# First batch's keys and values in six sets of 96 positions, q products in quarter tiles, idle products half as many, and a new set of ordering draws

## The chip, the core and the metric

The kernel runs on one core of a Trainium2 chip. Five engines work side by side, each through its own list of instructions in order, and meet at semaphores: TensorE (PE, matrix products into PSUM), VectorE (DVE), ScalarE (ACT), GpSimd (POOL) and SyncE (SP, which here only starts transfers). Sixteen DMA engines move data between HBM and SBUF. The metric is the device time of one execution in microseconds (us). Times named "us into the span" count from the first instruction of the profiled execution.

## The reference

Eight batches of eight heads, 576 positions, head dimension 64, all in float32. Attention without a softmax, an RMS norm per head, then four experts of two layers whose outputs are weighted by normalised probabilities and added up:

```python
def _attn_ref(q, k, v, g_norm) -> np.ndarray:
    kv = np.einsum('bhsd,bhse->bhde', k, v)
    out = np.einsum('bhsd,bhde->bhse', q, kv)
    rms = np.sqrt(np.mean(out * out, axis=-1, keepdims=True) + 1e-06)
    return (out / rms * g_norm).astype(np.float32)
...
    p = domain_probs / (domain_probs.sum(-1, keepdims=True) + 1e-09)
    out = np.zeros((N, D), dtype=np.float32)
    for e in range(E):
        h = np.maximum(x @ w1[e], 0.0)
        out += p[:, e:e + 1] * (h @ w2[e])
```

Here x has N = 4608 rows (8 x 576) of D = 512, w1 is 4 x 512 x 1024 and w2 is 4 x 1024 x 512. The sum over positions in `kv` has no order, so the 576 positions of a head may be cut into sets in any way, as long as k and v are cut alike.

## The kernel before

**Stages.** The rows are worked on in nine chunks of 512: the first 512 positions of each batch, and one chunk made of the 64 left over from each. Four experts times nine chunks make 36 steps s. Step s holds the first layer of one chunk (`up`, for s = 0 `up_plain`) and, beside it, the second layer (`down`, `down_deep`) of the chunk before. Most of these products are built with Strassen-like sums of blocks, which DVE and POOL form (line 563) and which ACT and DVE gather (lines 1432, 1440, 1760, 1768). All layer products are issued by one helper, `halves_of` (line 540): one product is split into two of 64 columns of weights each.

**How instructions show.** A float32 product stands in the trace as two weight loads (PEld) and two MATMUL records (PE), so 18 products of a source line are 36 records of each kind. A transpose through PE is one record of each kind.

**The opening (`opening`, line 860 on).** The first batch has a path of its own, since nothing else can run yet. It goes through four pairs of heads, hp = 0 to 3. For each:

- q, k and v of the pair are loaded by three transfers of 288 KB on SP's queue. All have the two heads one above the other on the 128 partitions: partition 64 h + p holds the nine positions 9 p to 9 p + 8 of head h, 9 x 64 numbers.
- `turns` (line 890): four transposes of q into an `ab` bank, which ACT copies out (line 895).
- `key_values` (line 905): nine sets of 64 positions; for each set one product per head, 64 rows by 64 columns, so 18 products, head 0 in the upper left quarter of the array and head 1 in the lower right. They gather in two banks, one `u2` and one `u1`. A last transpose (line 909) turns the ninth set of q. ACT and DVE copy the result out (lines 924, 921).
- `attend` (line 944), called twice: q times kv. For pairs 0 and 1 a call is eight products with 64 columns of weights (quarter tiles); for pairs 2 and 3 it is four products with 128 columns (`wide`). The result lies in halves of the two `db` banks (kind `raw`).
- `scaled`: squares on ACT (line 819), their sum on DVE (826), root and inverse (786 to 798), scaling on DVE (838); then four transposes back (`turn_x`, line 964), and ACT copies them out as a quarter of chunk 0 (line 970).

`up_plain` is the first layer of chunk 0 for expert 0, in the plain way: eight results i = 0 to 7, each gathering four pairs hp in one of the `u1` and `u2` banks, with 512 moving columns (the records "128x512"). Results 0 to 3 may begin as soon as pair 0 is there. The attention of the later batches (`attention`) loads k and v as 120 and 96 positions per set (`rows_of`); its products stand in line 1092, those with q in line 1117, the sums of squares in 1159 and 1165.

**Idle products.** Before the first data lands and in gaps of the opening up to key -1.99, PE runs `idle` (line 1921) on the identity matrix: four products of 64 x 64 x 64 into a free `ab` bank.

**Order.** The order of all instructions on all engines is worked out before the program is emitted, by a planner (`Plan`) in Python. Each operation has a key (its place in the steps), a cost per engine in us, and a due time. The planner runs a model of the engines, the transfers and the buffers, and at each moment an engine takes the operation that is due first among those that are ready. Due times are shifted by pseudo-random draws; `DEALS` names, for each step, the numbers of the draws that apply. An operation on a `raw` half waits in the model for others on these halves (`op.halves`, `seen`, `filled`). None of these numbers is read by the chip: they only set the order in which each engine's list is written.

**Weights.** Each expert's w1 and w2 are loaded while the expert before still runs. From expert 1 on some sums of weights are formed by ACT negating a block (line 636) and a transfer that adds HBM data on top.

Of the kernel before, what the change touches and what calls it, by code (L numbers as in the profile page):

```python
# [26 lines left out]
class Op:  # L27
    def __init__(self, key, cost, fn, reads, writes, kb, port):
        self.key, self.cost, self.fn, self.kb, self.port = key, cost, fn, kb, port
        self.outs = list(writes)  # L30
        self.bufs = list(dict.fromkeys(list(reads) + self.outs))
        self.deps = {}
        self.start = self.end = self.eng = None
        self.marks = self.seed = None
        self.wide, self.wants = {}, 0
        self.early = self.gang = self.opens = False
        self.halves = any(b.kind == "raw" for b in self.bufs)
# [5 lines left out]
class Plan:  # L43
# [20 lines left out]
    SLOW = 6.5  # L64
    SPREADS, SPREADS_PE, SHARES = (1.0, 2.0, 4.0), (0.0, 0.5, 1.5), (1.0, 0.2, 0.05)
# [42 lines left out]
    def prepare(self, slots, later, idle, idle_banks, idle_until):  # L108
# [50 lines left out]
        self.seen = self.filled = 0.0  # L159
# [74 lines left out]
    def ready(self, op, eng, front):  # L234
# [37 lines left out]
    def run(self, until):  # L272
# [3 lines left out]
        while self.left:  # L276
# [6 lines left out]
            for eng in todo:  # L283
# [35 lines left out]
                if eng == "PE" and busy[eng] <= t and 1.6 <= t and front < idle_until:  # L319
# [3 lines left out]
                    if spare is not None:  # L323
# [4 lines left out]
                        busy[eng] = op.end  # L328
# [14 lines left out]
    def begin(self, op, eng):  # L343
# [19 lines left out]
        if op.halves and eng == "PE":  # L363
            self.filled = max(self.filled, op.end)
        elif op.halves:
            self.seen = max(self.seen, op.end)
# [49 lines left out]
def kernel(  # L416
# [387 lines left out]
    def scaled(key, name, raw, n, x, blocks, by_half=False):  # L804
# [11 lines left out]
        for r in range(2):  # L816
# [6 lines left out]
            )  # L823
# [9 lines left out]
        for r in range(2):  # L833
# [19 lines left out]
            )  # L853
        return done

    x_part = [Buf(None, f"x0_{hp}") for hp in range(NPAIR)]
    opened = []

    def opening(key, span, rem):
# [9 lines left out]
        J = S // D  # L869
        qTs, kvs, lefts = {}, {}, []  # L870
        for hp in range(NPAIR):
            n = f"{b}_{hp}"
            loaded = {}
            for t, src, kb in zip("qkv", (q, k, v), (
                    (172, 194, 290), (183, 150, 150), (237, 400, 150), (172, 150, 172))[hp]):
                loaded[t] = Buf("big", f"{t}{n}")
                load(
                    key - 1 + 0.1 * hp, loaded[t], lambda t=loaded[t]: t.ap[:, 0:J * D],
                    src[b, 2 * hp:2 * hp + 2].rearrange("h (p j) d -> (h p) (j d)", j=J), kb,
                )  # L880
# [11 lines left out]
            plan.add(at(hp), {"PE": 0.54}, turns, reads=[qt], writes=[bank])  # L892
# [8 lines left out]
            def key_values(eng, bank=kbank, kt=kt, vt=vt, qt=qt):  # L901
                for j in range(J):
                    for r in range(2):
                        half, cols = slice(r * D, (r + 1) * D), slice(j * D, (j + 1) * D)
                        nc.tensor.matmul(  # L905
                            bank[r].ap[half, 0:D], lhsT=kt.ap[half, cols], rhs=vt.ap[half, cols],
                            start=(j == 0), stop=(j == J - 1), skip_group_check=True,
# [3 lines left out]
            plan.add(at(hp), {"PE": 1.3}, key_values, reads=[qt, kt, vt], writes=kbank)  # L911
# [38 lines left out]
            plan.add(  # L950
                at(hp + 0.4), {"PE": 0.26 if wide == D else 0.52}, attend, reads=[qT, kv_own], holds=[kv], writes=[raw])
            plan.add(
                at(hp + 0.4), {"PE": 0.26 if wide == D else 0.52}, lambda eng, attend=attend: attend(eng, other=1),
                reads=[qT, kv_other], holds=[kv], parts=[raw])
# [11 lines left out]
            plan.add(at(hp + 1), {"PE": 0.64}, turn_x, reads=[x], writes=[bank])  # L966
# [8 lines left out]

        n = f"{b}_r"
# [3 lines left out]
        def attend_rem(eng):  # L980
# [9 lines left out]
            at(NPAIR), {"PE": 1.07}, attend_rem,  # L990
            reads=list(kvs.values()) + list(qTs.values()) + lefts, writes=rawr)
# [11 lines left out]
        plan.add(at(NPAIR + 1), pe(4, P, 1), turn_xrem, reads=[xr], writes=[xb])  # L1003
# [16 lines left out]
    def attention(b, key, span, rem):  # L1020
# [26 lines left out]
        for s in range(2):  # L1047
# [64 lines left out]
            def attend(eng, raw=raw, rest=rest, kv=kv, qt=qt):  # L1112
# [9 lines left out]
            plan.add(  # L1122
                at(2 * s + 1.0), {"PE": 1.23}, attend, reads=[qt, kv], writes=raw + rest,
                early=True, gang=True,
            ).wide = {**{b: FIRST for b in raw}, **{b: S - FIRST for b in rest}}
# [29 lines left out]
        def total(eng):  # L1155
# [15 lines left out]
        plan.add(  # L1171
            when, {"PE": 1.23}, total, reads=both + [xs], writes=[ss]).wide = {ss: wide}
# [315 lines left out]
    def up_plain(s, e, c, key, span):  # L1488
# [4 lines left out]
        for i in range(8):  # L1493
            uh, a, u = i // 4, i // 2 % 2, i % 2
            bank = Buf("u1" if a == 0 else "u2", f"up{s}_{i}")
            for hp in range(NPAIR):
# [3 lines left out]
                def product(eng, w=w, bank=bank, dh=dh, kt=kt, ut=2 * a + u):  # L1500
# [9 lines left out]
                    **({"parts": [bank], "after": begun} if hp else {"writes": [bank]}),  # L1510
# [407 lines left out]
    def idle(bank):  # L1918
        for r in range(4):
            half = slice(r % 2 * D, (r % 2 + 1) * D)  # L1920
            nc.tensor.matmul(bank[half, 0:D], lhsT=ident[half, half], rhs=ident[half, half])  # L1921
# [54 lines left out]
```

## Time and profile before

| | |
|---|---|
| median of 3 runs | 1638.32 us (1638.09 to 1638.54) |
| the profiled execution, device time | 1638.29 us |
| its span, first to last instruction | 1636.5 us |
| PE busy | 1627.3 us, 99% of the span |
| DVE busy | 1317.3 us, 80% |
| ACT busy | 971.9 us, 59% |
| POOL busy | 625.7 us, 38% |
| mean granted TensorE clock | 0.999 |

A group in the profile gives line, engine, operation, what is written and read, shapes, count, and the busy time; in brackets stands the idle time before it and what ended it. The chain of waits follows the work that ended last back to the start: its rows give start, length in us, and the engine, tile and line. In a table by stages a row is the stretch, its length, the busy time, the count, the granted clock, the busy share of the DMA engines and GB/s. MATMUL records are pipelined, and each one's length holds some 0.2 us of its way through the array, so the pace is read from start to start (as in the chain), not from the mean of one.

### The profile page before, as it was taken

How to read it: one execution, taken by the hardware profiler on the slowest of the kernel's cores; microseconds unless marked ns; L12 is line 12 of the kernel's file. 1: busy time of each engine (PE TensorE's matmuls, PEld its weight loads, DVE VectorE, ACT ScalarE, POOL GpSimd, SP SyncE). 2: the span in 40 equal slices, each digit the busy share in tenths (PEclk: the TensorE clock that was granted, in tenths of full speed). 3: DMA queues.
4: the chain of work that ended last, by engine and by line, in shares of the span. 5: the costliest groups of instructions: out<-in, count | busy, mean ns of one | idle time of the engine just before them, and what ended most of it. 6: DMA issues, size and time to landing. Idle time of an engine off the chain costs nothing.

```text
span 1636.5 us, 66139 instructions
## 1 busy us (share of the span) xinstructions
PE 1627.3 (99%) x28692; PEld 1555.0 (95%) x28692; DVE 1317.3 (80%) x2211; ACT 971.9 (59%) x2462; POOL 625.7 (38%) x618
## 2 busy tenths in 40 slices
PE   9999999999999999999999999999999999999999
PEld 5698889888999999999999999999999999999997
DVE  6877777788889878977988887778889877787776
ACT  4465555565566666656666665665666666566653
POOL 4122424333343454433354533344254443333332
PEclk9999999999999999999999999999999999999999
DMA  9888777744764435444675543334577544444442
GB/s 234 225 186 248 183 215 209 173 147 173 236 166 131 118 95 154 118 108 116 181 178 136 130 111 102 116 104 118 144 186 181 120 113 118 118 115 108 118 105 53
DMA packets 225596, 240.96 MB, mean 147 GB/s; under 512 B 100890, under 2 KB 165274, under 8 KB 225306
## 3 DMA queue, kind: packets, MB, share of 16 engines
q1 hardware_dynamic: 201690, 199.96, 40.4%
q0 software_dynamic: 23616, 36.78, 15.0%
q8 instruction: 225, 3.69, 0.9%
q14 instruction: 65, 0.53, 0.1%
HBM read 162.21 MB, written 74.47 MB: 145 GB/s over the span
## 4 chain that ended last, share of the span: by engine, by line
PE 97%; DMA 1%; DVE 1%; SPq 0%; issue 0%; ACT 0%; POOL 0%; DVEq 0%; POOLq 0%; ACTq 0%
PE u L540 47%; PE db L540 31%; PE ab L540 15%; PE ab L1092 1%; DMA big<-in_moe_w_dram 1%; PE ab L1117 1%; PE ab L1159 0%; PE db L1117 0%; DMA big<-roots 0%; SPq L569 0%; PE u L905 0%; PE ab L1921 0%; PE db L944 0%; DVE xf L563 0%; DMA small<-in_q_dram 0%
## 5 line engine op out<-in xcount | busy, mean ns | idle before, releaser
L563 DVE TENSOR_TENSOR big<-big,big 128x256 f32<-128x256 f32 (+1 forms) x522 | 478.2, 932 | 28.1 <-ACT big L1396 13.6
L540 PE MATMUL u<-xf,big 128*64 128x128 f32 x6784 | 493.8, 273 | 0.0
L540 PE MATMUL db<-big,big 128*64 128x128 f32 (+1 forms) x5648 | 434.0, 290 | 0.4 <-DVE big L563 0.4
L540 PEld LDWEIGHTS u<-xf,big 128*64 128x64 f32 x6784 | 398.7, 137 | 2.9 <-issue 0.8
L540 PE MATMUL u<-xf,w1y 128*64 128x128 f32 x5304 | 395.4, 273 | 0.1
L540 PEld LDWEIGHTS db<-big,big 128*64 128x64 f32 x5648 | 339.8, 137 | 25.3 <-DVE big L563 0.9
L540 PEld LDWEIGHTS u<-xf,w1y 128*64 128x64 f32 x5304 | 313.5, 137 | 5.1 <-issue 1.0
L563 POOL TENSOR_TENSOR big<-big,big 128x256 f32<-128x256 f32 (+1 forms) x162 | 187.4, 1158 | 255.6 <-DVE big L563 110.6
L1440 DVE TENSOR_TENSOR big<-u,snap 128x256 f32<-128x256 f32 x440 | 185.2, 421 | 122.9 <-PE u L540 81.1
L1432 ACT ACTIVATE snap<-u 128x256 f32<-128x256 f32 x490 | 187.1, 382 | 161.9 <-PE u L540 142.1
L1432 ACT ACTIVATE big<-u 128x256 f32<-128x256 f32 x440 | 167.4, 382 | 71.8 <-PE u L540 54.0
L563 POOL TENSOR_TENSOR big<-big 128x512 f32<-128x512 f32 (+1 forms) x82 | 100.8, 1230 | 193.8 <-DVE big L563 99.2
L1760 ACT ACTIVATE snap<-db 128x256 f32<-128x256 f32 (+1 forms) x256 | 90.0, 352 | 106.1 <-PE db L540 88.2
L1396 ACT ACTIVATE big<-big 128x1024 f32<-128x1024 f32 x125 | 131.7, 1054 | 13.1 <-DVE big L563 7.6
L563 DVE TENSOR_TENSOR big<-big 128x512 f32<-128x512 f32 (+1 forms) x160 | 122.3, 772 | 2.4 <-PE db L540 1.2
L1768 DVE TENSOR_TENSOR big<-ab,snap 128x256 f32<-128x256 f32 x168 | 70.9, 422 | 63.9 <-ACT snap L1760 43.9
L1432 ACT ACTIVATE u<-u 128x256 f32<-128x256 f32 x245 | 90.7, 370 | 52.7 <-PE u L540 39.3
L1605 POOL DMA_DIRECT2D out_dram<-big x104 | 93.8, 1229 | 36.5 <-ACT big L1581 23.1
L540 PE MATMUL ab<-kv,big 128*64 128x128 f32 x1504 | 104.6, 273 | 0.0
L540 PE MATMUL ab<-big,big 128*64 128x128 f32 (+1 forms) x1384 | 96.9, 275 | 0.0
L540 PEld LDWEIGHTS ab<-kv,big 128*64 128x64 f32 x1504 | 87.2, 137 | 0.0
L540 PEld LDWEIGHTS ab<-big,big 128*64 128x64 f32 x1384 | 80.5, 137 | 1.2
(213 smaller groups left out, 2231.1 us busy)
## 6 DMA issues: line engine op xcount, KB each, us to landing
xf<-x SPq DMA_DIRECT2D x104, 512.0 KB, 3.6
xf<-x_h SPq DMA_DIRECT2D x85, 256.0 KB, 3.3
xf<-x SPq DMA_DIRECT2D x78, 256.0 KB, 3.8
x<-xf SPq DMA_DIRECT2D x36, 512.0 KB, 4.4
out_dram<-big POOLq DMA_DIRECT2D x68, 256.0 KB, 6.1
big<-in_moe_w_dram SPq DMA_DIRECT2D x30, 512.0 KB, 5.8
big<-in_moe_w_dram POOLq DMA_DIRECT2D x18, 512.0 KB, 7.6
x_h<-big SPq DMA_DIRECT2D x17, 512.0 KB, 4.1
```

The lines of the kernel that those rows point to most:

```text
L540: nc.tensor.matmul(out_[cols], lhsT=lhsT[:, cols], rhs=rhs, **kw)
L563: lambda eng: adder(eng).tensor_tensor(out=out_(), in0=a(), in1=b(), op=op),
L1092: nc.tensor.matmul(bank.ap[o * D:(o + 1) * D, r * D:(r + 1) * D], lhsT=ks[r], rhs=vs[r], start=(j == r == 0), stop=(j == len(sets[0]) - 1) ...
L1117: nc.tensor.matmul(to[o].ap[cols, 0:width], lhsT=kv.ap[half, cols], rhs=qt.ap[half, r * S + at_:r * S + at_ + width],)
L1396: lambda eng: nc.scalar.activation(out=b.ap[:], in_=b.ap[:], func=ACT.Relu),
L1432: lambda eng: nc.scalar.activation(out=where(), in_=ps.ap[:, 0:HN], func=ACT.Copy),
L1440: lambda eng: nc.vector.tensor_tensor(out=block(whole, a, t), in0=src.ap[:, 0:HN], in1=add_.ap[:], op=ALU.add),
L1605: nc.gpsimd.dma_start(out=dst, in_=cell(i)[parts, :], accum_op=ALU.add)
L1760: lambda eng: nc.scalar.activation(out=where(), in_=group_of(ps.ap), func=ACT.Copy),
L1768: lambda eng: nc.vector.tensor_tensor(out=cell(tq, dq), in0=group_of(src.ap), in1=group_of(add_.ap), op=ALU.add,),
```

## The change

Five things change.

- k and v of the first batch are loaded as six sets of 96 positions: partition p of 96 holds positions 6 p to 6 p + 5 of both heads, side by side. q is loaded as before.
- `key_values` follows: six sets, two heads, 12 products of 96 rows by 64 columns instead of 18 of 64 by 64.
- `attend` uses products with 64 columns of weights for all four pairs.
- `idle` is one call of `halves_of`: two products of 128 rows, 64 columns of weights and 128 moving columns, instead of four of 64 x 64 x 64.
- The planner: costs of the opening's products are set anew; an operation on `raw` halves now waits for other engines' work on the same bank; going between the opening's kinds of products and the others costs 0.11 us in the model (`SWITCH`, `turns`); results 1 and 3 of `up_plain` begin after the last pair's `key_values` (`first_kv`); and `DEALS` holds other draws for steps -3 to 15 and for 22, 23, 29 and 32.

```diff
-        -3: (61,), -2: (96, 339), -1: (17, 340), 0: (41, 337, 607, 846, 1010), 1: (145, 260, 617, 782,
...
+        -2: (178,), -1: (141,), 0: (175, 256, 724, 986, 1100), 1: (79, 362, 728, 792, 1183), 2: (54, 360,
...
-        if op.halves:
-            when = max(
-                when, self.seen + self.TO_PE if eng == "PE" else self.filled + self.AFTER_PE)
+        for bank in op.halves:
+            for e, end in self.halved[bank].items():
+                if e != eng:
+                    when = max(when, end + (
+                        self.AFTER_PE if e == "PE" else self.TO_PE if eng == "PE" else self.OTHER))
...
+            if eng == "PE":
+                op.end += self.SWITCH[op.turns] if op.turns != self.turned else 0.0
+                self.turned = op.turns
...
-        J = S // D
+        J, SETS = S // D, 6
+        ROWS = S // SETS
...
+                else:
+                    load(
+                        key - 1 + 0.1 * hp, loaded[t],
+                        lambda t=loaded[t]: t.ap[0:ROWS, 0:2 * SETS * D].rearrange(
+                            "p (h x) -> p h x", h=2),
+                        heads.rearrange("h (p j) d -> p h (j d)", j=SETS), kb,
+                    )
...
-                for j in range(J):
+                for j in range(SETS):
                     for r in range(2):
-                        half, cols = slice(r * D, (r + 1) * D), slice(j * D, (j + 1) * D)
+                        half, at = slice(r * D, (r + 1) * D), (r * SETS + j) * D
                         nc.tensor.matmul(
-                            bank[r].ap[half, 0:D], lhsT=kt.ap[half, cols], rhs=vt.ap[half, cols],
-                            start=(j == 0), stop=(j == J - 1), skip_group_check=True,
+                            bank[r].ap[half, 0:D], lhsT=kt.ap[0:ROWS, at:at + D],
+                            rhs=vt.ap[0:ROWS, at:at + D],
+                            start=(j == 0), stop=(j == SETS - 1), skip_group_check=True,
                         )
...
-            raw, wide = Buf("raw", f"raw{n}"), D if hp < 2 else P
+            raw, wide = Buf("raw", f"raw{n}"), D
...
-                    **({"parts": [bank], "after": begun} if hp else {"writes": [bank]}),
+                    **({"parts": [bank], "after": begun} if hp else {
+                        "writes": [bank], "after": first_kv if i in (1, 3) else ()}),
...
     def idle(bank):
-        for r in range(4):
-            half = slice(r % 2 * D, (r % 2 + 1) * D)
-            nc.tensor.matmul(bank[half, 0:D], lhsT=ident[half, half], rhs=ident[half, half])
+        halves_of(bank[:, 0:P], ident[:], rhs=ident[:])
```

More of the change, by code (lines that the diff above doesn't have):

```diff
@@ L36, in __init__ @@
         self.early = self.gang = self.opens = False
-        self.halves = any(b.kind == "raw" for b in self.bufs)
+        self.halves, self.turns = (), False
 BANKED = ("u1", "u2", "db", "ab")
@@ L327, in run @@
                         op.fn = lambda eng, bank=self.slots[kind][spare[1]]: idle(bank)
-                        busy[eng] = op.end
+                        busy[eng], self.turned = op.end, False
                         self.free[kind].remove(spare)
@@ L362, in begin @@
             self.worked += op.cost[eng]
[L363 to L366, printed above, removed]
+        for bank in op.halves:
+            self.halved[bank][eng] = max(self.halved[bank].get(eng, 0.0), op.end)
         if op.port:
@@ L822, in scaled @@
                 reads=[raw[r][0]], parts=[x],
-            )
+            ).halves = (r,) if by_half else ()
         plan.add(
@@ L948, in attend @@
                             )
[L950 to L954, printed above, removed]
+            for other, own in enumerate((kv_own, kv_other)):
+                op = plan.add(
+                    at(hp + 0.4), {"PE": 0.27},
+                    lambda eng, attend=attend, other=other: attend(eng, other=other),
+                    reads=[qT, own], holds=[kv], **{"parts" if other else "writes": [raw]})
+                op.halves, op.turns = (0, 1), True
             x = Buf("big", f"xg{n}")
@@ L1169, in total @@
                     )
-        plan.add(
-            when, {"PE": 1.23}, total, reads=both + [xs], writes=[ss]).wide = {ss: wide}
+        op = plan.add(when, {"PE": 1.13}, total, reads=both + [xs], writes=[ss])
+        op.turns, op.wide = True, {ss: wide}
         def root(eng):
```

37 lines of the change are left out of this document (22 added, 15 removed), and 10 rows, old and new, of the table DEALS.

## The prediction

> **What bounds the kernel now.** I read the page first: its busy times, then the chain of waits by engine.
>
> ```profile
> PE 1627.3 (99%) x28692; PEld 1555.0 (95%) x28692; DVE 1317.3 (80%) x2211; ACT 971.9 (59%) x2462; POOL 625.7 (38%) x618
> ...
> PE 97%; DMA 1%; DVE 1%; SPq 0%; issue 0%; ACT 0%; POOL 0%; DVEq 0%; POOLq 0%; ACTq 0%
> ```
>
> TensorE holds 97% of the chain, so the time is PE's work plus its few gaps. The view of PE's own waits lists the gaps whole:
>
> ```profile
> PE db L540 <- ACT ab L1760: 2.1, 1, 2.1
> PE ab L1921 <- POOL ident masks.py:199: 1.4, 1, 1.4
> PE u L905 <- issue: 1.0, 1, 1.0
> PE db L540 <- DVE big L563: 0.4, 1, 0.4
> ```
>
> Together 4.9 us. The change lies in the opening, so next I read the chain there, in order of time (start, length, engine, tile, line, count).
>
> ```profile
> 1.37 2.40 PE ab L1921 x40
> 3.77 1.06 PE ab L890 x4
> 4.83 1.48 PE ab L1921 x24
> 6.31 1.18 PE u L905 x36
> ...
> 7.93 0.58 PE ab L890 x4
> 8.52 0.62 PE db L944 x32
> 9.14 1.05 PE u L905 x36
> ...
> 10.86 0.73 PE db L944 x30
> 11.59 0.10 PE u L905 x3
> 11.69 1.03 issue
> 12.72 1.15 PE u L905 x33
> ...
> 14.54 1.08 PE db L944 x16
> ...
> 16.20 1.01 PE u L540 x4
> 17.21 0.59 PE ab L964 x4
> 17.80 1.19 PE u L905 x36
> ...
> 20.23 0.59 PE db L944 x8
> ...
> 21.41 0.59 PE db L944 x8
> ...
> 36.13 1.17 PE ab L1092 x40
> ```
>
> Until 6.1 us PE waits for data and idles on purpose (L1921). From there every piece is needed work, laid end to end, save one hole of 1.03 us. So a microsecond of work taken out between 6 and 22 us moves all that follows up, as long as what follows has its data. That is the question of this change.
>
> **Keys times values (terms 1).** The four calls of L905 took 1.18, 1.05, 0.10 + 1.15 (with the hole between) and 1.19 us, 1.17 on average for 36 records. The new form, 96 rows by 64 columns, is that of a later batch: L1092 with 40 records of 120 and 96 rows took 1.17, so 29.3 ns each, and 24 records cost 0.70. The first of the four ran partly before PE was at speed, so I average the three clean whole values 1.18, 1.05 and 1.19 to 1.14: 4 x (1.14 - 0.70) = 1.76 us saved. Bounds: against 1.05 it is 1.40, against 1.19 it is 1.96.
>
> **q products in quarters (terms 2).** Pair 2 took 1.08 for 16 records of 64 by 128, pair 3 0.59 + 0.59 = 1.18. In quarters a pair takes twice the records, 32, but took 0.62 (pair 0). Saved: 0.46 + 0.56 = 1.02 us. With pair 1's 0.73 for 30 it is 0.80.
>
> **Idle products.** L1921 shows 64 records where the code has four products, two records each: eight rounds. Two products make half the records, 32, not a quarter. They fill waits for loads: a shorter or longer round changes only when PE is free at q's or v's landing, by at most one round, 2.40 / 5 = 0.48 us. They also wake the clock: the first transposes took 1.06 where later ones took 0.58, so if the new form wakes it later or sooner I allow 0.5 us either way. I cost both at nothing, covered by the loads.
>
> **The hole of 1.03 us.** It stands within one call of L905, after three of 36 records, so no semaphore explains it; the view says "issue". The page has a queue for code (packets, MB, share of the DMA engines):
>
> ```profile
> q8 instruction: 225, 3.69, 0.9%
> ```
>
> 3.69 MB in 225 packets is 16.4 KB each; PE has 2 x 28692 records, 255 per packet. I take the hole for a late packet of code: it comes after 221 MATMUL records, when the loads have filled the DMA engines (second table below). The change cuts 32 idle and twice 12 L905 records ahead of that place, 56 in all, so the same place in the code comes 56 records later: the rest of pair 2's L905 (21), its transposes (5) and 30 of the 32 quarter records of its L944. The packet then has some 2 us more to arrive, but quarter records use up code fastest (32 in 0.62 us). Between 0 and 1.03 saved, I take half: 0.5. [...]
>
> **Loads of k and v.** Eight transfers keep their bytes but go to 96 partitions in 192 pieces instead of 128 in 128. I read the table by stages for PE, and the landing times in the first 22 us:
>
> ```profile
> 5.00:10.00 5.00, 5.00 (x137) 4.63 (x135) 0.74 (x4) 2.38 (x7) 0.00 (x0) 1.00 0.97 335
> 10.00:15.00 5.00, 3.97 (x94) 3.37 (x90) 3.78 (x14) 3.04 (x12) 0.73 (x1) 1.00 1.05 400
> 15.00:20.00 5.00, 5.00 (x65) 2.94 (x62) 3.51 (x13) 3.02 (x8) 2.34 (x4) 1.00 1.06 246
> ...
> big<-in_v_dram SPq DMA_DIRECT2D x4, 288.0 KB, 5.3
> ```
>
> The engines are full (0.97, 1.05, 1.06). The eight carry 8 x 288 KB = 2.36 MB, 5.9 us at 400 GB/s. Nothing here shows a load of this size on 96 partitions. Lower bound: no change, 0. Upper: the 246 GB/s of the next stage at the same share, 9.6 us, so 3.7 later for the last. I take 0, since most pieces of 2304 B become 1536 B, far nearer to the big pieces of the 400 GB/s row than to the 128-byte pieces of q that fill the slow row. [...]
>
> **Order.** The new draws cost no work, they move it. PE's gaps after 22 us are 2.1 and 0.4, so an ideal order gains 2.5; a worse one meets new waits like the 2.10, and I allow two more, 4.2. I take 0. The added rule that results 1 and 3 of L540 follow the last L905 adds no wait on the chip (PE's list is in order anyway): it leaves two of the four results to fill PE before 17 us, of which the present order uses one group of 1.01. The waits between engines on `raw` banks and the 0.11 us of a switch exist in the planner's model only.
>
> **Sum.** 1.76 + 1.02 + 0.5 = 3.28 us less. The profiled execution took 1638.29 us (span 1636.5, 1.8 around it), 0.03 under the median of 1638.32, so both give **1635.0 us**.
>
> **Rivals.**
>
> A, more goes away. The largest gap of PE is a chain of lateness that has nothing to do with the opening, except that the new order moves everything:
>
> ```profile
> 844.73 10.67 DMA big<-in_moe_w_dram
> ...
> 855.42 1.06 ACT L636 ACTIVATE big<-big 128x1024 f32<-128x1024 f32 x1 [2.64 <-DMA big<-in_moe_w_dram]
> ...
> 857.08 1.09 PE L540 MATMUL db<-kv,big 128*64 128x128 f32 x16 [2.10 <-ACT ab L1760]
> ...
> big<-in_moe_w_dram SPq DMA_DIRECT2D x30, 512.0 KB, 5.8
> ```
>
> A weight block landed after 10.67 us where the median is 5.8; ACT's negation L636 stood at the head of its list, the copies L1760 behind it came late, and PE waited. If that goes and the hole goes whole: 1638.29 - 2.78 - 1.03 - 2.10 = 1632.4. Against it: the same transfers stay.
>
> B, the gain is lost at 60 us. There PE waits for DVE, and DVE before that for the w2 loads:
>
> ```profile
> 45.61 0.42 DVE L563 TENSOR_TENSOR w2y<-big 128x256 f32<-128x256 f32 x1 [1.52 <-DMA big<-in_moe_w_dram]
> 47.63 1.23 DVE L563 TENSOR_TENSOR big<-big,big 128x1024 f32<-128x1024 f32 x1 [1.59 <-DMA big<-in_moe_w_dram]
> ...
> 25.00:50.00 25.00, 19.73 (x41) 1.00 1.08 223
> 50.00:60.00 10.00, 9.83 (x19) 1.00 0.56 187
> ...
> 60.04 3.67 PE L540 MATMUL db<-big,big 128*64 128x256 f32 x32 [0.42 <-DVE big L563]
> ```
>
> In the table by stages for DVE the DMA engines are full until 50 us (1.08), then DVE is (9.83 of 10). PE coming 3.3 us sooner would find the same sums unready and wait 3.3 longer: 1638.3. Against it: DVE idled 1.52 + 1.59 us for loads whose place in SP's queue the order may change, and 9.83 us hold sums not needed first.
>
> C, slower through the loads. If 96 of 128 partitions stretch a load by 128/96, the eight take 5.9 x 1/3 = 2.0 us more on full engines; all behind them lands later, w2 included, and by B's wall the end moves 2.0 later in spite of the work saved: 1640.3, and 1642.0 with the 3.7. It decides once the stretch outweighs what slack DVE has before 60 us.
>
> D, slower through late weights. A's mechanism, several times: three experts' weights come by six such negations each, and one in eighteen stalled. Four more at 2.10 against 3.28 gained give 1638.29 - 3.28 + 8.4 = 1643.4; from the second on it is slower than before.
>
> **How the numbers follow.** Forecast 0.45, own range 1633.8 (hole gone, both terms at their upper bounds, 0.5 for the clock) to 1636.6 (hole kept, lower bounds, 0.5 the other way); A 0.18, B 0.15, C 0.12, D 0.10. What a measurement of this kernel can tell from no change is about 0.2%, 3.3 us: 1635.0 and 1641.6. The forecast lies on that line: 0.27 below it, 0.18 within. A is below, B within, C 0.05 within and 0.07 above, D 0.01 and 0.09. So faster 0.45, same 0.39, slower 0.16. The range runs from 1631.8 (A with the 0.4 gap gone too and 0.2 off the terms' upper bounds) to 1642.0 (C's far end); left out are D's upper part and little else.
>
> **What would show it.** L905's successor: 24 records a pair in 0.70 us. L944: 32 records a pair, none of 64 by 128, 0.62. L1921's successor: some 32 records. The first L540 record about 2 us before 16.2. A hole marked "issue" near 14 us would halve the third term's case; none would prove it. For B: a wait of PE on DVE near 57 to 60 us of 3 us. For C: landings of v well above 5.3 us and GB/s below 335 in the stage from 5 to 10. For A and D: PE's waits on ACT or DVE in the hundreds of us, at the steps where weights change. The forecast is wrong if L1092's pace doesn't hold for the new form, or if the time stands between 1637 and 1641 with the opening shorter.

## The result, and the profile after

| | before | after |
|---|---|---|
| median, 22 executions each | 1638.43 us (1636.76 to 1641.71) | 1641.87 us (1638.21 to 1645.22) |
| ratio after / before, 95% | | 1.0016 [1.0009, 1.0022] |
| the same in a second series, 27 and 11 executions | 1639.76 us | 1640.31 us, 1.0008 [1.0000, 1.0017] |
| and in a third | 1639.30 us | 1642.28 us, 1.0016 [1.0007, 1.0025] |
| the profiled execution and its span | 1638.29 us, 1636.5 us | 1638.46 us, 1636.6 us |

By the ratio of 1.0016 the change costs 2.6 us, by the medians 3.4. The forecast of 1635.0 us is wrong, in sign too. The profiled execution of after is among the fastest of its 22. It shows what went wrong in the opening, but not the whole loss; a second profile of the same kernel (run e11 below, 1643.4 us of span) shows more.

Line numbers moved: transposes of q L890 are now L905, keys times values L905 are L920, the q products L944 are L961, the transposes back L964 are L982, the layer products L540 are L544, batch 1's keys times values L1092 are L1111, and the copies L1760 are L1781.

The page of after, busy times:

```profile
PE 1627.9 (99%) x28644; PEld 1553.1 (95%) x28644; DVE 1313.5 (80%) x2203; ACT 975.1 (60%) x2462; POOL 639.1 (39%) x626
```

The count has fallen by 48: 4 x 12 records fewer of keys times values, 32 more of q products, 32 fewer of idle ones. PE's busy time has not fallen with them: it rose by 0.6 us. Work was taken out and what is left ran slower.

The chain of waits of after in the opening (start, length, engine, tile, line, count):

```profile
1.68 5.29 DMA big<-in_v_dram
...
7.10 1.55 PE u L920 x24
...
10.80 0.86 PE u L920 x23
...
15.84 0.76 PE db L961 x23
16.59 0.62 issue
17.21 0.36 PE db L961 x2
...
18.62 2.96 PE u L544 x8
...
22.16 0.85 PE u L920 x24
...
23.68 0.62 PE db L961 x32
```

Before, the chain ran through PE from 1.37 us on, with one hole of 1.03 us. Now it begins with a load of v: the first products of keys and values start at 7.10 instead of 6.31 us. The first eight records of the layer (18.62) take 2.96 us, and the first layer record comes 2.4 us later than the 16.20 of before, where I had put it 2 us sooner. PE's own waits in after (us in total, times, longest), and the row of the first products in the timeline, which names their wait:

```profile
PE db L544 <- ACT ab L1781: 1.1, 1, 1.1
PE u L920 <- DMA big<-in_v_dram: 0.8, 1, 0.8
PE db L961 <- issue: 0.6, 1, 0.6
```

```profile
7.10 1.55 PE L920 MATMUL u<-big,big 96*64 96x64 f32 x24 [0.77 <-DMA big<-in_v_dram]
```

The table by stages (length; busy time and count of PE, PEld, DVE, ACT, POOL; granted clock; DMA share; GB/s), and the landing of v in the first 22 us:

```profile
5.00:10.00 5.00, 4.23 (x49) 3.41 (x51) 0.45 (x2) 1.30 (x5) 0.00 (x0) 1.00 1.05 288
10.00:15.00 5.00, 4.77 (x124) 4.01 (x121) 2.83 (x11) 3.51 (x11) 0.34 (x1) 1.00 1.09 314
15.00:20.00 5.00, 4.24 (x44) 2.44 (x44) 3.49 (x13) 2.80 (x8) 1.84 (x3) 0.74 1.05 340
20.00:25.00 5.00, 5.00 (x75) 2.83 (x73) 1.45 (x6) 2.26 (x7) 2.17 (x3) 0.92 0.79 113
```

```profile
big<-in_v_dram SPq DMA_DIRECT2D x4, 288.0 KB, 7.2
```

Three things stand here that before did not have. The transfers run at the same full share of the engines but move 288 and 314 GB/s where they moved 335 and 400; v's median landing is 7.2 us, not 5.3. PE gets through 49 records in the stage from 5 to 10 us, not 137. And the granted clock, 1.00 before, falls to 0.74 and 0.92: (1 - 0.74) x 5 x 2 + (1 - 0.92) x 5 x 2 = 3.4 us at half rate, which is what made the eight layer records take 2.96 us (the same eight take 1.87 in e1 below). The trace has this stretch itself, granted 0.5 from 17.38 to 20.79 us into the span, 3.41 us; a stretch of this length is the "window" in the expectation of e1.

The trace also shows something that the table hides. Its rows of granted clock begin at 10.55 us, in before at 6.48; up to there the table writes 1.00 because no row says otherwise. The pace says otherwise: 24 records of L920 take 1.55 us at 7.10 and 0.85 at 22.16. So in this execution PE was also slow for some 4 us longer at the start.

### The profile page after: what moved, and what is told of

It is laid out like the page before. It is cut to its first block, busy times and chain, and to the rows that moved or that the text cites. A ratio compares the mean times of both kernels' runs of the same rounds, so it can differ in the third digit from the quotient of the medians.

```text
span 1636.6 us, 66038 instructions
## 1 busy us (share of the span) xinstructions
PE 1627.9 (99%) x28644; PEld 1553.1 (95%) x28644; DVE 1313.5 (80%) x2203; ACT 975.1 (60%) x2462; POOL 639.1 (39%) x626
## 4 chain that ended last, share of the span: by engine, by line
PE 99%; DMA 0%; DVE 0%; issue 0%; ACT 0%; SPq 0%; DVEq 0%; ACTq 0%
PE u L544 48%; PE db L544 32%; PE ab L544 15%; PE ab L1111 1%; PE ab L1136 1%; PE ab L1179 0%; PE db L1136 0%; DMA big<-in_v_dram 0%; PE u L920 0%; PE db L961 0%; PE ab L905 0%; PE ab L982 0%; PE ab L1185 0%; PE db L1003 0%; SPq L573 0%
## 5 line engine op out<-in xcount | busy, mean ns | idle before, releaser
L544 PE MATMUL u<-xf,big 128*64 128x128 f32 x6784 | 494.7, 273 | 0.0
L567 DVE TENSOR_TENSOR big<-big,big 128x256 f32<-128x256 f32 (+1 forms) x489 | 449.3, 935 | 30.0 <-ACT big L1416 14.3
L544 PE MATMUL db<-big,big 128*64 128x128 f32 (+1 forms) x5576 | 427.5, 290 | 0.0
L544 PEld LDWEIGHTS u<-xf,big 128*64 128x64 f32 x6784 | 398.3, 137 | 4.0 <-issue 1.9
L544 PE MATMUL u<-xf,w1y 128*64 128x128 f32 x5304 | 395.8, 273 | 0.0
L544 PEld LDWEIGHTS db<-big,big 128*64 128x64 f32 x5576 | 334.0, 137 | 25.0 <-ACT snap L1781 0.3
L544 PEld LDWEIGHTS u<-xf,w1y 128*64 128x64 f32 x5304 | 312.7, 137 | 3.4 <-issue 1.2
L567 POOL TENSOR_TENSOR big<-big,big 128x256 f32<-128x256 f32 (+1 forms) x163 | 194.0, 1191 | 232.7 <-DVE big L567 94.7
L567 POOL TENSOR_TENSOR big<-big 128x512 f32<-128x512 f32 (+1 forms) x75 | 93.2, 1243 | 170.9 <-DVE big L567 123.7
L1781 ACT ACTIVATE snap<-db 128x256 f32<-128x256 f32 (+1 forms) x256 | 90.3, 353 | 112.4 <-PE db L544 96.3
L1789 DVE TENSOR_TENSOR big<-ab,snap 128x256 f32<-128x256 f32 x174 | 73.4, 422 | 65.8 <-ACT snap L1781 44.9
L1626 POOL DMA_DIRECT2D out_dram<-big x118 | 105.0, 1227 | 40.0 <-ACT big L1602 30.4
L544 PE MATMUL ab<-kv,big 128*64 128x128 f32 x1488 | 103.4, 273 | 0.0
L1602 ACT ACTIVATE big<-big,p_all 128x256 f32<-128x256 f32 x200 | 92.9, 501 | 5.5 <-DVE big L1820 4.8
L544 PE MATMUL ab<-big,big 128*64 128x128 f32 (+1 forms) x1336 | 93.9, 275 | 0.0
L544 PEld LDWEIGHTS ab<-kv,big 128*64 128x64 f32 x1488 | 86.3, 137 | 0.0
```

The lines of the kernel that those rows point to most:

```text
L544: nc.tensor.matmul(out_[cols], lhsT=lhsT[:, cols], rhs=rhs, **kw)
L567: lambda eng: adder(eng).tensor_tensor(out=out_(), in0=a(), in1=b(), op=op),
L1602: lambda eng: nc.scalar.activation(out=cell(i, half), in_=ap(), func=ACT.Copy, scale=prob()),
L1626: nc.gpsimd.dma_start(out=dst, in_=cell(i)[parts, :], accum_op=ALU.add)
L1781: lambda eng: nc.scalar.activation(out=where(), in_=group_of(ps.ap), func=ACT.Copy),
L1789: lambda eng: nc.vector.tensor_tensor(out=cell(tq, dq), in0=group_of(src.ap), in1=group_of(add_.ap), op=ALU.add,),
```

## The experiments

All kernels up to e9 keep the planner's order of the kernel that they start from; only what an operation issues differs. The last five, e11 apart, change the order on purpose. "Before" is the kernel before on the same chip in the same series, 27 executions; an experiment has 10 or 11, e5 and e6 one each.

**e1: the loads and products of before in the order of after.** In the kernel after:

```diff
-                if t == "q":
+                if True:
...
-                for j in range(SETS):
+                for j in range(J):
...
-                        half, at = slice(r * D, (r + 1) * D), (r * SETS + j) * D
+                        half, cols = slice(r * D, (r + 1) * D), slice(j * D, (j + 1) * D)
...
-                            bank[r].ap[half, 0:D], lhsT=kt.ap[0:ROWS, at:at + D],
-                            rhs=vt.ap[0:ROWS, at:at + D],
-                            start=(j == 0), stop=(j == SETS - 1), skip_group_check=True,
+                            bank[r].ap[half, 0:D], lhsT=kt.ap[half, cols], rhs=vt.ap[half, cols],
+                            start=(j == 0), stop=(j == J - 1), skip_group_check=True,
```

> The changed kernel with its own order of instructions, but the first batch's k and v loaded on 128 partitions again and multiplied in nine sets of 64. Load theory (96 partitions stretch the eight loads, v of the last pair lands at 14.8 us instead of 16.9, PE's first wait on v goes and the clock wakes a window sooner): the products cost 4 x 0.44 = 1.8 us more, the loads give back 2.2 and the clock some 1.7, so about 2 us faster than the changed kernel's 1641.9, near 1639.8; first keys-times-values products at 6.3 us instead of 7.1. Order theory (the new order is the loss, the loads are hidden): 1.8 us slower than the changed kernel, 1643.7.

**e3: the opposite, six sets on 96 partitions in the order of before.** In the kernel before, the edit of the change to the loads and to `key_values`, and nothing else:

```diff
-        J = S // D
+        J, SETS = S // D, 6
+        ROWS = S // SETS
...
+                        lambda t=loaded[t]: t.ap[0:ROWS, 0:2 * SETS * D].rearrange(
+                            "p (h x) -> p h x", h=2),
+                        heads.rearrange("h (p j) d -> p h (j d)", j=SETS), kb,
...
```

> The kernel before with its own order and its own planner costs, but k and v in six sets of 96. Load and clock theory: slower than before by 0.5 to 2.5 us although the products cost 1.8 less, 1639 to 1641; v of the last pair lands at 16.9 us, PE waits about 0.8 us on v ahead of the first products. Order theory: 1.8 us faster than before, 1636.6.

Measured: e1 1639.45 us against 1639.16, ratio 1.0004 [0.9995, 1.0014]; e3 1642.31 against 1639.16, 1.0017 [1.0007, 1.0026]. So the six sets alone cost 3.15 us in the old order (1.1 to 4.3 by the interval), about what the whole change costs, and without them no loss of the new order is clear. The stages of e1 for PE alone:

```profile
5.00:10.00 5.00, 4.93 (x121) 1.00 1.01 360
10.00:15.00 5.00, 3.72 (x88) 1.00 1.04 399
```

360 and 399 GB/s are back, and 121 records in the first stage. In e3 PE's waits and stages show the same illness as after:

```profile
PE db L540 <- ACT ab L1771: 2.1, 1, 2.1
PE u L915 <- DMA big<-in_v_dram: 1.7, 1, 1.7
```

```profile
5.00:10.00 5.00, 5.00 (x107) 1.00 1.05 293
10.00:15.00 5.00, 3.34 (x76) 0.95 1.07 306
15.00:20.00 5.00, 5.00 (x28) 0.50 1.06 342
20.00:25.00 5.00, 5.00 (x53) 0.87 0.68 103
```

A wait of 1.7 us on v, and then (0.05 + 0.50 + 0.13) x 5 x 2 = 6.8 us at half rate.

**e6 and e5: is it the spread over the partitions, or the smaller pieces?** e6 loads each pair's k and v as one piece of 3072 bytes on each of 96 partitions, which mixes the positions of the two heads and so changes the output, but not the work; e5 goes back to 128 partitions as in e1, but in 384 pieces of 768 bytes. Each was run once.

```diff
-                        lambda t=loaded[t]: t.ap[0:ROWS, 0:2 * SETS * D].rearrange(
-                            "p (h x) -> p h x", h=2),
-                        heads.rearrange("h (p j) d -> p h (j d)", j=SETS), kb,
+                        lambda t=loaded[t]: t.ap[0:ROWS, 0:2 * SETS * D],
+                        heads.rearrange("h (p j) d -> (h p) (j d)", j=2 * SETS), kb,
```

```diff
+                        (lambda t=loaded[t]: t.ap[:, 0:768].rearrange("p (c x) -> p c x", c=3)[:, :, 0:192]),
...
+                        heads.rearrange("h (p c j) d -> (h p) c (j d)", c=3, j=3), kb,
...
```

> The changed kernel, but the eight loads of k and v fill their 96 partitions with one piece of 3072 B each instead of two of 1536 B; bytes, partitions, products and order are the same (the positions get mixed between sets and heads, so the output isn't the reference's). If the spread over 96 partitions stretches the loads, v of the last pair still lands at 16 to 17 us. If the pieces do, it lands by 14.8 us, as in the kernel before.

> As the nine-set kernel (128 partitions, the changed kernel's order), but each load of k and v in 384 pieces of 768 B. Tells what stretches the loads. If the spread over partitions does (two thirds of the bytes on partitions 0 to 63), these land as the nine-set kernel's, v of the last pair at 14.8 us. If the smaller pieces do (192 of 1536 B), these are worse still, v of the last pair at 17 us or later.

Measured: 1638.81 us (e6) and 1638.11 us (e5). PE's stages, e6 first, then e5:

```profile
5.00:10.00 5.00, 4.04 (x92) 1.00 1.05 280
10.00:15.00 5.00, 4.48 (x112) 1.00 1.04 305
```

```profile
5.00:10.00 5.00, 4.59 (x104) 1.00 1.01 330
10.00:15.00 5.00, 3.79 (x102) 1.00 1.08 362
```

A landing time counts from the issue, which differs between kernels, so I also took from the packets of each trace when the last of the four v is in, in us into the span:

| kernel | partitions x piece | GB/s 5 to 10, 10 to 15 | last v in at |
|---|---|---|---|
| before | 128 x 2304 B | 335, 400 | 14.75 |
| e1 | 128 x 2304 B | 360, 399 | 14.32 |
| after | 96 x two of 1536 B | 288, 314 | 16.9 |
| e6 | 96 x 3072 B | 280, 305 | 17.35 |
| e5 | 128 x three of 768 B | 330, 362 | 16.02 |

Pieces larger than those of before do not help on 96 partitions (e6), so the spread alone is enough to stretch the loads, by 2.2 (after against before) to 3.0 us (e6 against e1) at the end of the eight. With pieces of 768 B on 128 partitions the last v is in 1.7 us later than in e1; its load was also issued 0.8 us later (8.86 against 8.08 us), so a price of small pieces is likely here and its size open. That after's 1536 B add anything of their own, nothing here shows. Each of e5 and e6 is one execution, so their times decide nothing; the landings do.

**e9: fewer bytes on the same 96 partitions.** The kernel after with four of the six sets loaded; the products of the last two sets use the first two again.

```diff
+                        lambda t=loaded[t]: t.ap[0:ROWS, 0:2 * SETS * D].rearrange(
+                            "p (h x) -> p h x", h=2)[:, :, 0:4 * D],
...
+                        half, at = slice(r * D, (r + 1) * D), (r * SETS + j % 4) * D
```

> The changed kernel with only four of the six sets of k and v loaded, still on 96 partitions; the last two sets' products run on the first two again (so the output isn't the reference's). Same products, order and idle products, two thirds of the bytes of the eight loads. Load theory: v of the last pair lands before 14.8 us, PE's waits on v go, the saved work shows: 1 to 2.5 us faster than the changed kernel on the same chip and no slower than before. Order theory, or a loss in the products: no change against the changed kernel, 1 to 3 us over before.

Measured: 1639.84 us, 1.0001 [0.9992, 1.0010], where after on the same chip (e11) took 1642.28: 2.4 us went with a third of the bytes. Its stages for PE and its chain of waits in the opening:

```profile
5.00:10.00 5.00, 5.00 (x103) 1.00 1.08 282
10.00:15.00 5.00, 4.16 (x97) 1.00 1.07 315
```

```profile
6.41 1.04 PE u L920 x24
...
8.12 0.62 PE db L961 x32
8.74 0.90 PE u L920 x24
```

The same products in the same order start at 6.41 instead of 7.10, and pair 1's at 8.74 instead of 10.80. The transfers are as slow as in after, 282 and 315 GB/s, but with a third fewer bytes v is there in time.

**e2: is it the clock?** After, with two more idle products ahead of the first pair's products, so that PE's clock wakes while v is on its way.

```diff
...
+                for i in range(2 if hp == 0 else 0):
+                    halves_of(bank[0].ap[:, 0:P], ident[:], rhs=ident[:])
```

> The changed kernel with two more rounds of idle products in PE's list ahead of the first keys-times-values products, 0.86 us for a wait of 0.77. Clock theory (that wait keeps PE's clock at half rate until 10.6 us instead of 6.5): the clock wakes near 7.1 us in most executions, 3.4 us of half rate saved, 1.7 us faster than 1641.9 and less scatter between executions. Load theory alone, or order theory: no change, or 0.1 us slower.

Measured: 1641.24 us, 1.0013 [1.0003, 1.0024], where after has 1.0016 in the first series: no clear gain, and not the 1.7 us expected. PE's stages and waits:

```profile
15.00:20.00 5.00, 4.23 (x54) 1.00 1.06 336
20.00:25.00 5.00, 5.00 (x67) 1.00 0.87 132
```

```profile
PE db L544 <- ACT ab L1783: 2.9, 1, 2.9
PE u L544 <- DVE big L1462: 1.4, 3, 0.6
PE ab L1113 <- DMA big<-in_v_dram: 1.2, 1, 1.2
```

The rows of granted clock begin at 7.80 us instead of 10.55 and stay at 1.00, as meant, and yet hardly anything came of it: this execution lost 2.9 + 1.4 + 1.2 us further on. That was a miss, and it pointed away from the opening alone.

**e4 and e8: the idle products and the quarters.** e4 is after with the old four idle products. e8 is before with quarters for all pairs and the new idle products, and nothing else.

```diff
-        halves_of(bank[:, 0:P], ident[:], rhs=ident[:])
+        for r in range(4):
+            half = slice(r % 2 * D, (r % 2 + 1) * D)
+            nc.tensor.matmul(bank[half, 0:D], lhsT=ident[half, half], rhs=ident[half, half])
```

```diff
-            raw, wide = Buf("raw", f"raw{n}"), D if hp < 2 else P
+            raw, wide = Buf("raw", f"raw{n}"), D
...
```

> The changed kernel with the idle products of before, four of 64 x 64 x 64, which puts 32 more MATMUL records ahead of the first keys-times-values products. Code theory (PE stops where its code runs into a block that has not yet come): the hole marked issue stays at the 222nd MATMUL record from the start, as in the kernel before and in the changed one, which is now 32 records earlier in the work: within the third pair's keys-times-values or its transposes, near 14.8 us, not in its products with q at 16.6. If the hole belongs to the products with q, it stays with them. The time: 1641.9 as the changed kernel if the form of the idle products doesn't matter; 1640 or less if the new form is what keeps the clock at half rate.

> The kernel before with its own order, loads and nine sets, and two parts of the change alone: the q products in quarters for all four pairs, and the short idle products. If what PE saves in the opening reaches the end, 1.0 us faster than before by the quarters, and the hole of 1.03 us moves 16 records on or shrinks: 1636.4 to 1637.4 where before is 1638.4. If later waits swallow it, no change.

> The changed kernel once more, on one chip with the next. Its median near 1641.9 and 2.6 us over the kernel before. Clock theory: in this execution too PE's clock wakes later than the 6.5 us of before, or falls back to half rate within the first 25 us, and each such stretch of 3.4 us costs about 1.7 us by the time the opening is over.

Measured on one chip: e4 1644.29 us, 1.0023 [1.0012, 1.0033]; e8 1639.24, 0.9999 [0.9990, 1.0008]; after again (e7) 1640.31, 1.0008 [1.0000, 1.0017]. PE's waits in e4, then in e8:

```profile
PE ab L1111 <- DMA big<-in_v_dram: 2.4, 1, 2.4
...
PE ab L982 <- issue: 0.5, 1, 0.5
```

```profile
PE u L905 <- issue: 1.0, 1, 1.0
PE ab L1092 <- DMA big<-in_v_dram: 1.0, 1, 1.0
```

e4 settles the place of the hole: with the 32 idle records back it moves to the transposes L982, 32 records earlier in the code, that is, to the 222nd MATMUL record again. It is the 222nd in fifteen of the sixteen traces; in e3 PE is there so late that no gap shows. It is a place in the instruction stream, not in the program's work.

What PE waits for there can be read from the packets. The first packet of 16 KB in the span on the queue for code lands at 11.36 us in before and at 15.80 in after, and the hole ends 1.4 us later in both. In all fifteen traces it ends 1.26 to 1.54 us after this packet. Where the packet is early against PE (e14, landed at 12.53, PE at the place at 13.82) the hole is 0.2 us; where it starts to move only 0.5 us before PE gets there (e10), 1.8. That ties the hole to a late packet of code; whose code it holds, the trace does not say.

That the old idle products cost anything is not shown. Against e7 they cost 4.0 us, but the intervals of the two overlap, and against the 1.0016 of after's other two series it is 1.1 us. e4's executions lie in two groups, four from 1639.5 to 1641.1 us and six from 1644.2 to 1646.2. The profiled one is of the first; it waits 2.4 us for batch 1's v at L1111, and behind that the clock is at half rate from 46.36 to 49.77 us. e8 shows where a gain in the opening ends: L1092, keys times values of batch 1, waits 1.0 us for its v at about 42 us, which it did not do before. e8's interval, 1.6 us under before to 1.3 over, does not exclude the 1.0 us that was expected, either.

**e10 to e14: late weights.** The longest wait of PE after the opening is the one near 857 us, where ACT's negation (L640; L636 in before) waits for a block of w1. e11 is after once more, profiled beside e9. In e10 (e8), e12 (after), e13 (before) and e14 (e1) the planner's assumed landing time of weight blocks from expert 1 on is 11.0 us instead of 6.7, in both weight loads. That number is read by the planner alone; it makes the order ask for the blocks earlier or use them later.

```diff
-                w1_src(e, dh, uh), 512 if e else (300, 300, 344, 450)[i], also=[corner[n]], lands=6.7,
+                w1_src(e, dh, uh), 512 if e else (300, 300, 344, 450)[i], also=[corner[n]], lands=11.0 if e else 6.7,
...
-                w2_src(e, uh, dh), 512 if e else 330, also=[corner[n]], lands=6.7,
+                w2_src(e, uh, dh), 512 if e else 330, also=[corner[n]], lands=11.0 if e else 6.7,
```

> The changed kernel once more, on one chip with the two others: 0.5 to 3 us over before, since it was 3.4 over in the first series of runs and 0.6 in the second.

> The kernel with quarters and short idle products in the order of before, with one number of the planner changed: it takes 11.0 us instead of 6.7 for a block of the next expert's weights to land, as the late block of before took 10.67. A try for a faster version: if PE's wait near 857 us (1.1 to 2.9 us in all profiles so far) goes, 1 to 2 us faster than before, 1637 to 1638 where before is 1639; if the late block only moves, no change.

> The changed kernel with the planner's 11.0 us for the landing of the next experts' weights. Two-place theory (the changed kernel loses in the opening through its loads, and again near 857 us, where PE's wait on ACT behind a late weight block reached 2.8 and 2.9 us and in one profile let the clock fall to half rate for 6.8 us): the second loss goes, 2 to 4 us faster than the changed kernel, within 1 us of before. If the loads of the opening are the whole loss: no change, 2 to 3 us over before.

> The kernel before with the 11.0 us alone, without the quarters and the short idle products. If the landing time is what made the faster version faster: 1637.5 where before is 1639.3, 1.8 us faster, as with the quarters. If the quarters do it: no change against before.

> The changed kernel's order with nine sets on 128 partitions and the 11.0 us. If the two losses add: 2 us faster than the changed kernel with the 11.0 us alone, and 1 to 2 us faster than before. If what comes after the opening swallows the loads' share: as the changed kernel with the 11.0 us.

| | median us | ratio to before on the same chip |
|---|---|---|
| e11, after | 1642.28 | 1.0016 [1.0007, 1.0025] |
| e10, e8 + 11.0 | 1637.52 | 0.9989 [0.9981, 0.9998] |
| e12, after + 11.0 | 1639.65 | 1.0002 [0.9993, 1.0011] |
| e13, before + 11.0 | 1637.53 | 0.9992 [0.9982, 1.0001] |
| e14, e1 + 11.0 | 1636.44 | 0.9986 [0.9977, 0.9995] |

The stages of e11 and e12 around the wait, PE alone, and in e11 the row of the negation in ACT's timeline:

```profile
855.00:860.00 5.00, 3.32 (x62) 1.00 1.14 234
860.00:865.00 5.00, 3.81 (x36) 0.54 1.10 238
865.00:870.00 5.00, 5.00 (x76) 0.78 0.58 119
```

```profile
859.53 1.06 ACT L640 ACTIVATE big<-big 128x1024 f32<-128x1024 f32 x1 [3.41 <-DMA big<-in_moe_w_dram]
```

```profile
855.00:860.00 5.00, 5.00 (x98) 1.00 1.12 233
860.00:865.00 5.00, 5.00 (x96) 1.00 1.14 285
865.00:870.00 5.00, 5.00 (x96) 1.00 1.05 234
```

In e11 ACT waits 3.41 us for the block and PE, behind it, 2.9; then the clock runs at half rate for (0.46 + 0.22) x 5 x 2 = 6.8 us: the 96 to 98 records of a stage fall to 36 and 76. In e12 all of it is gone. What is left of PE's waits in e12, and those on keys times values in e14:

```profile
PE ab L1111 <- DMA big<-in_v_dram: 1.7, 1, 1.7
PE u L920 <- DMA big<-in_v_dram: 1.6, 3, 0.9
PE u L544 <- DVE big L1460: 1.5, 3, 0.7
...
PE db L961 <- issue: 1.3, 1, 1.3
```

```profile
PE u L920 <- DMA big<-in_v_dram: 0.2, 1, 0.2
PE u L920 <- issue: 0.2, 1, 0.2
```

e12 and e14 differ only in the loads and products of keys and values: 3.3 us of waits on v against 0.2, and 1639.65 - 1636.44 = 3.2 us of time. The hole adds to it (1.3 us against 0.2), and e14 has a wait of 1.0 us on ACT at L905 of its own. The slowest of e14's eleven executions took 1637.94 us, the fastest of e12's 1638.18. That is the 3.15 of e3 once more, with the late weights out of the way. e14 is faster than both kernels of the case; the lead over before, 2.5 us, is 0.14% [0.05%, 0.23%].

**The loss, put together.** Six sets of 96: +3.2 us net (e3; e12 against e14), about the whole loss. It is there by 46 us, at the second call of keys times values of batch 1, here in after and in e1:

```profile
45.50 1.39 PE L1111 MATMUL ab<-big,big 120*64 120x64 f32 x40
```

```profile
42.54 1.26 PE L1110 MATMUL ab<-big,big 120*64 120x64 f32 x34
```

With nine sets in this order the call is under way at 42.5 and 42.6 us (e1, e14), with two thirds of the bytes at 42.6 (e9), with six sets at 44.4 to 46.5 (after, e2, e4, e6, e7, e11, e12), whether the clock fell on the way (after, e7) or not (e11, e12). In the old order it is 44.9 against 41.5 (e3, before). The late weights: after's ratios of 1.0016, 1.0008 and 1.0016 fall to 1.0002 in e12, some 1.0 to 2.3 us; before has this loss too, 1.45 us (e13, whose interval ends at no change), so that after loses more by them than before is not shown. Quarters and idle products: nothing clear (e8, 0.9999). Draws and costs of the planner: nothing clear (e1 against e8, 1.0004 and 0.9999 in two series).

**Where the scatter comes from.** Each execution has its mean granted clock. All executions on record with their clock, of before in four series and of after in three, in groups:

| mean clock | before, 108 executions | after, 44 executions |
|---|---|---|
| 1.000 | 47%, median 1638.29 us | 20%, median 1640.08 us |
| 0.999 | 32%, 1640.04 us | 36%, 1640.61 us |
| 0.998 and less | 20%, 1641.60 us | 43%, 1643.05 us |

After is later in each group, and more of its executions have lost clock. The share at 1.000 rises to 8 of 11 in e12 and 9 of 11 in e14.

## Why the prediction was wrong

**The step that failed is the loads of k and v, taken as 0** with bounds of 0 and 3.7 us. I judged by the size of the pieces; the runs show that on 96 partitions even larger pieces are late (e6). The last v came 2.2 us later in the profile of after, and the net price of the six sets is 3.2 us with the saving of term 1 already in it. The bound of 3.7 us, from the 246 GB/s row, holds the landing. I gave the forecast to the row that looked nearest. Rival C's stretch comes close in size: 2.0 us by it, 2.2 (after) to 3.0 (e6 against e1) measured at the last v. Its factor of 128/96 was an assumption that no run shows: the GB/s of the two stages from 5 to 15 us fell from 335 to 288 and from 400 to 314, by factors of 1.16 and 1.27. By what way the spread slows the packets, no trace shows.

**Rival C was right** in that the eight loads stretch on 96 partitions (after, e6), in its price at the loads and nearly in its time: 1640.3 us against 1638.29 x 1.0016 = 1640.9. Its signs, v above 5.3 us (7.2) and fewer than 335 GB/s (288), are there. Everything behind these loads lands later, as it said, but the time is lost to batch 1's v (L1111) and to the clock and not, as it said, at DVE's wall near 60 us: no wait of PE on DVE stands there in after. That its sum came within 0.6 us is in part luck, since it gave that wall all the saved work. What it lacked is what went with the late v in the profile of after: PE idles 0.77 us, and the clock wakes 4.1 us later (10.55 us against 6.48) and falls for 3.4 us. The loss does not need the clock, though: e12 is at full clock from 6.58 us to the end and its median still 3.2 us behind e14's.

**Term 1, mis-sized.** Keys times values take 0.85 us for 24 records ("22.16 0.85", at full clock), 35 ns each and not the 29.3 of L1092's mixture of 120 and 96 rows. Saved are 4 x (1.14 - 0.85) = 1.16 us, not 1.76, and below my lower bound of 1.40. The forecast named this as what would make it wrong.

**Term 2, q products in quarters, right in size** where PE runs at full clock: 0.62 us for 32 records. That the gain reached the end is not shown: in e8 the time did not clearly fall.

**The hole.** Its place was predicted exactly: the chain has 23 records of L961 in a row, then the gap, then two, and by count it is the 222nd MATMUL record, after 30 of the 32. That it would cost half was not borne out: 0.62 in this profile, 1.3 in e1, e7, e11 and e12, 0.2 in e14. It depends on when the packet of code comes: that landed at 11.36 us in before and at 15.80 in after, later with all the rest, so the 56 records did not buy the time that I took them to buy. The longest hole, in e10, was 1.8 us.

**Idle products, costed at nothing.** Not settled: after with the old ones (e4) is 4.0 us slower than e7 on the same chip, 1.1 by the ratios of the other two series, with intervals that overlap; before with the new ones and quarters (e8) is no different.

**Order, costed at nothing:** nothing clear against it (e1, e8). The wait of D, behind the negation near 857 us, cost PE 2.1 us before and 1.1, 2.8 and 2.9 us in three profiles of after, so not "four more" waits but one that varies, and in e11 costs clock too.

**Rival B** is right that a gain can meet a wall of loads, at another place than I put it: not DVE at 60 us but v of batch 1 at 42 to 46 us (L1092 in e8 1.0 us, L1111 in e11 and e12 1.4 and 1.7; none in the first profile of after). The DMA engines are full until 50 us, 1.08 before and 1.10 in after. **Rival A** needs the late weights and the hole to go; e12 is the first half of that: 1.0002, not 1632.4.

The range, 1631.8 to 1642.0, holds the median of 1641.87 at its very edge; the chance of 0.45 on faster did not come true.

**What stays open:** whether the form of the idle products costs anything; what on the chip the spread over 96 partitions slows; why the clock falls in some executions of a kernel and not in others with the same waits (in e2 it stayed at 1.00 after a wait of 2.9 us near 860); and how the late weights share between waiting and clock, since each kernel has one profile, after three.

## What to carry to other kernels

Before a load is reshaped to suit the matrix products, ask what it does to the transfer: 96 partitions instead of 128 cost more at full DMA engines than a third fewer products gave back, here 3.2 us net. A saving in an opening that runs on data still landing is only worth what the next landing allows (in e8 batch 1's v, with a wait of 1.0 us); look at the wait after the next before adding up terms. And where the forecast lies within the scatter of executions, take the late waits out first (here one planner number): the executions then lie closer together, within 2.9 us in e12 where e11 has 5.7, within 2.5 in e14 where e1 has 6.5.

## What the runs showed of the hardware that was not expected

- With the DMA engines full, 272 to 320 GB/s were moved from 5 to 15 us in the nine traces with k and v on 96 partitions, 335 to 400 in the six with 128 and pieces of 2304 B. Pieces of 3072 B were no help on 96 (e6: 280 and 305).
- A short starvation of PE can cost more than itself: 0.77 us on v and the hole of 0.62 went with 3.41 us at half clock in after, a wait of 2.9 us with 6.83 us at half clock in e11, and with none in e2. These are one and two times 3.41, and in after the granted clock changes at 10.55, 17.38 and 20.79 us, two and one times 3.41 apart. What sets this length, no run told.
- The hole "issue" of 0.2 to 1.8 us stands at one fixed MATMUL record of the stream, the 222nd, whatever the kernel does there, and ends 1.26 to 1.54 us after a 16 KB packet of code has landed.
- Products of 96 rows by 64 columns issue every 35 ns here, slower than a mixture of 120 and 96 rows elsewhere (29.3 ns). The rows are not the whole reason: in e1, 64 rows by 64 columns took 1.26 us for 36 records in one pair and 1.03 for 35 in the next, 35 and 29 ns each. No run told why.
